# Window attention before two MLPs: scores of 64x64 blocks on quarters of the array

## The chip, the cores and the metric

One core of a Trainium2 chip (trn2). Its engines are TensorE (PE in the profile, with its weight loads as PEld), VectorE (DVE), ScalarE (ACT), GpSimd (POOL) and SyncE (SP, whose queue issues nearly all transfers here). Matmul results go to PSUM, 8 banks of 128 partitions by 512 fp32 columns; only PE, DVE and ACT reach it. The metric is device microseconds of one execution.

## The reference

Sliding-window attention (batch 4, 8 heads, 576 positions, head size 64, window 64), then two MLPs over the 2304 tokens, 512 to 2048 to 512 wide. The first MLP's activation is the square of the positive part, the second's is ELU. All in fp32.

```python
scores = (1 / sqrt(64)) * q @ k.T
rel = pos[:, None] - pos[None, :]
scores = where((rel >= 0) & (rel < 64), scores, -1e9)
attn = exp(scores - max(scores)); attn = attn / (sum(attn) + 1e-9)
x = (attn @ v)            # heads side by side: [2304, 512]
x = square(maximum(x @ w_in1, 0)) @ w_out1
h = x @ w_in2
out = where(h > 0, h, exp(minimum(h, 0)) - 1) @ w_out2
```

## The kernel before, in words

The tokens are cut into five blocks `t` of 512, 256, 512, 512 and 512 (`BLOCKS`). The eight heads are taken as four pairs `p`; a *unit* `(t, p)` is one head pair in one block. `q` and `k` come with the two heads of a pair on partitions 0 to 63 and 64 to 127 (`D` = 64) and positions along the free dimension. A window of 64 queries (`WIN`) meets only the 128 keys that end with its own 64, so a block of 512 has 8 windows of 64 queries by 128 keys for each head.

**Loads** (`u_load`, line 327). q goes into a tile `qd` laid out in blocks on the diagonal: in window `b`, head `a` occupies its own 64 partitions and columns `a*64` to `a*64+63` and the rest is zero, so two transfers with 256-byte pieces bring it in. k keeps whole lines with 64 positions ahead of the block, v comes in two arrangements. `load_to` issues them on SP a unit ahead. There are two q tiles, `qd0` and `qd1`, one for even and one for odd pairs.

**Scores** (`u_S`, line 369). One product a window: the weights are the 128x128 block-diagonal q of both heads, the moving operand is the 128 keys, contracted over all 128 partitions. Four windows share a PSUM bank `pa` (pool `ps_a`, two banks; block 0 uses the four banks of `ps_o`). A 128x128 result holds one window: 64 queries of the first head above 64 of the second. DVE adds the mask and takes the minimum (`tensor_tensor_reduce`, shown as CUSTOM_DVE), ACT takes the exponential with its sum, and the rows are divided by their sums on DVE, in block 1 on ACT. `mask[1]` is the mask of a window that begins a sequence; the 64 keys before it belong to another sequence.

**Transposes and the product with V** (`u_T`, line 413; `u_PV`, line 426). Each 128x128 is transposed on PE and copied to `pt` by ACT; then each window and head has a product of 64 columns on one half of the array's columns (`pa<-pt,vr`, 128*64 in the profile). `u_V2` does this for two units one after the other.

**First MLP, blocks 0 to 2.** For each of 16 column blocks `j` of the hidden layer, `m_h` (line 471) makes the first product `ph` (12 matmuls; each operand is split in two fp32r parts and three of their products are summed) in a bank of pool `ps_h` (two banks); ACT applies Relu and Square, ACT and DVE split the result into `gs`; `m_out` (line 490) adds the second product into four accumulators `o` in `ps_o` (12 matmuls). The main loop (lines 924 to 969) writes `m_h` two steps ahead of `m_out`, and puts among them the units of the next block: those of block 1 in block 0's loop, those of block 2 in block 1's, and those of blocks 3 and 4 from the end of block 1's through block 2's. `decode` and `slot` put conversions of the weights (fp64 to split fp32, sums of quarters for a fast matrix product) on DVE and ACT in between. Blocks 3 and 4 and the second MLP follow with seven products in place of eight (`stepw`, `step`, `prod2`; banks `px` from `ps_h`, `py` from `ps_a`, `po` from `ps_o`).

**Order.** A planner that simulates the engines chooses the order of each engine's instructions from the program order and the dependencies, at build time; each engine then runs its own queue in order. `tc.issue_after(x)` keeps what is written within it behind `x` in that order. `last["pe"]` and its like remember instructions for this. A tile with the same `tag` takes the place of an older one and waits until that is no longer used.

## Time and profile before

| | us |
|---|---|
| median of 3 runs (lowest to highest) | 830.05 (828.53 to 830.63) |
| the profiled execution's own time | 830.28 |
| its span, first to last instruction | 828.5 |

| engine | busy us | share of the span | instructions |
|---|---|---|---|
| PE | 813.0 | 98% | 4908 |
| PEld | 743.3 | 90% | 4908 |
| DVE | 666.4 | 80% | 1747 |
| ACT | 571.8 | 69% | 1353 |
| POOL | 5.8 | 1% | 21 |

How to read the profile: the busy time of PE includes pipelined matmuls whose ends are modelled, so the starts of instructions are what is compared. Most DVE and ACT instructions go through one helper and stand under its line, 53; they are told apart by the tiles that they write and read, as `pb<-pa,mask`. Line 467 holds both products of the first MLP (`ph<-xs,w` and `o<-gs,w`), 379 the scores, 420 the transposes, 433 the product with V.

### The profile page before, as it was taken

The page shows a single profiled execution, that of the slowest core. Times are in us where ns is not written, and L with a number is a line of the kernel's source. Part 1 is how long each engine was busy: PE and PEld are TensorE (multiplying, and loading weights), DVE is VectorE, ACT ScalarE, POOL GpSimd, SP SyncE. Part 2 cuts the span into 40 slices and gives each one's busy share as a digit, 9 for nine tenths or more (in the row PEclk, how much of TensorE's full clock was granted, in tenths as well). Part 3 has the DMA queues.
Part 4 walks back from the last instruction along what each step waited for, and adds up shares of the span by engine and source line. Part 5 has one row for each costly group of instructions (what it writes and reads, how often), then busy time and mean ns, then how long its engine had stood idle before and what let it go on. Part 6 is the DMA issues. An engine that isn't in the chain of part 4 may idle for free.

```text
span 828.5 us, 14865 instructions
## 1 busy us (share of the span) xinstructions
PE 813.0 (98%) x4908; PEld 743.3 (90%) x4908; DVE 666.4 (80%) x1747; ACT 571.8 (69%) x1353; POOL 5.8 (1%) x21
## 2 busy tenths in 40 slices
PE   6899999999999999999999999999999999999998
PEld 5687889998888887888888899999999999999998
DVE  7999995999689898989994767699666898576875
ACT  6787975678678777887773567766477756577552
POOL 2000000000000000000000000000000000000000
PEclk9999999999999999999999999999999999999999
DMA  9997334759467669999988696878987877887832
GB/s 303 386 394 266 110 110 131 228 191 295 158 217 213 234 213 361 338 379 353 333 296 276 230 336 253 303 269 274 311 268 263 305 260 228 268 279 270 299 118 58
DMA packets 121613, 214.90 MB, mean 259 GB/s; under 512 B 46144, under 2 KB 68928, under 8 KB 113088
## 3 DMA queue, kind: packets, MB, share of 16 engines
q1 hardware_dynamic: 120704, 213.75, 75.6%
q8 instruction: 39, 0.64, 0.3%
q14 instruction: 38, 0.31, 0.1%
q10 hardware_dynamic: 832, 0.20, 0.1%
HBM read 160.43 MB, written 53.48 MB: 258 GB/s over the span
## 4 chain that ended last, share of the span: by engine, by line
PE 90%; DMA 6%; SPq 2%; ACT 2%; issue 0%; DVE 0%; ACTq 0%
PE o L467 22%; PE po L883 20%; PE px L685 14%; PE ph L467 12%; PE py L685 10%; PE po L685 6%; PE pa L379 3%; DMA wraw<-in_moe_w_out_dram 2%; PE pa L433 2%; PE pa L420 1%; DMA wd<-w 1%; PE px L883 1%; DMA wraw<-in_moe_w_in_dram 1%; DMA qd<-in_q_dram 1%; DMA wd<-tl 1%; SPq L342 0%
## 5 line engine op out<-in xcount | busy, mean ns | idle before, releaser
L467 PE MATMUL o<-gs,w 128*128 128x512 f32 (+1 forms) x960 | 216.3, 372 | 0.0
L467 PEld LDWEIGHTS o<-gs,w 128*128 128x128 f32 x960 | 166.4, 189 | 29.2 <-ACT gs L53 0.3
L883 PE MATMUL po<-g,wr 128*128 128x384 f32 (+1 forms) x972 | 168.6, 333 | 0.0
L883 PEld LDWEIGHTS po<-g,wr 128*128 128x128 f32 x972 | 167.4, 188 | 0.0
L467 PE MATMUL ph<-xs,w 128*128 128x512 f32 (+1 forms) x576 | 126.8, 361 | 2.8 <-ACT xs L53 2.2
L53 ACT ACTIVATE g<-gr 128x384 fp32r<-128x384 f32 x168 | 86.9, 524 | 55.5 <-PE po L883 49.6
L467 PEld LDWEIGHTS ph<-xs,w 128*128 128x128 f32 x576 | 94.9, 190 | 17.9 <-ACT xs L53 2.7
L53 DVE TENSOR_TENSOR g<-gr,g 128x384 fp32r<-128x384 f32 x168 | 90.0, 552 | 16.1 <-ACT g L53 15.1
L685 PE MATMUL px<-xo,wr 128*128 128x384 f32 x432 | 83.8, 334 | 0.0
L685 PEld LDWEIGHTS px<-xo,wr 128*128 128x128 f32 x432 | 75.8, 188 | 0.3
L53 ACT ACTIVATE sy<-px 128x384 f32<-128x384 f32 x69 | 33.8, 490 | 42.5 <-PE px L685 42.0
L53 DVE TENSOR_SCALAR y<-y 128x256 uint32<-128x256 uint32 (+4 forms) x162 | 55.7, 366 | 6.8 <-ACT y L53 6.2
L53 ACT ACTIVATE pb<-pb,nm 128x128 f32<-128x128 f32 x144 | 55.8, 391 | 4.2 <-DVE nm L53 4.0
L685 PE MATMUL po<-xo,wr 128*128 128x384 f32 x288 | 56.2, 334 | 0.0
L685 PE MATMUL py<-xo,wr 128*128 128x384 f32 x288 | 55.7, 334 | 0.0
L53 DVE TENSOR_TENSOR gr<-sy,py 128x384 f32<-128x384 f32 x48 | 26.6, 554 | 35.6 <-PE py L685 23.3
L53 DVE TENSOR_TENSOR gr<-gr 128x384 f32<-128x384 f32 x96 | 52.2, 553 | 0.5
L685 PEld LDWEIGHTS po<-xo,wr 128*128 128x128 f32 x288 | 50.5, 188 | 0.0
L685 PEld LDWEIGHTS py<-xo,wr 128*128 128x128 f32 x288 | 50.5, 188 | 0.0
L53 DVE TENSOR_TENSOR gs<-g,gs 128x512 fp32r<-128x512 f32 (+1 forms) x64 | 39.7, 621 | 11.7 <-ACT gs L53 11.2
L685 PE MATMUL px<-xo,w 128*128 128x512 f32 x192 | 46.6, 390 | 0.7 <-ACT tl L53 0.7
L685 PEld LDWEIGHTS px<-xo,w 128*128 128x128 f32 x192 | 36.0, 188 | 8.6 <-ACT tl L53 1.2
(91 smaller groups left out, 1205.0 us busy)
## 6 DMA issues: line engine op xcount, KB each, us to landing
wr<-wd SPq DMA_DIRECT2D x66, 1024.0 KB, 6.0
wr<-wd SPq DMA_DIRECT2D x24, 768.0 KB, 4.8
wd<-tl SPq DMA_DIRECT2D x59, 256.0 KB, 3.8
w<-wd SPq DMA_DIRECT2D x56, 256.0 KB, 5.1
wd<-wo SPq DMA_DIRECT2D x46, 256.0 KB, 4.9
wd<-xs SPq DMA_DIRECT2D x39, 256.0 KB, 3.0
wraw<-in_moe_w_in_dram SPq DMA_DIRECT2D x16, 512.0 KB, 8.3
vr<-in_v_dram SPq DMA_DIRECT2D x16, 512.0 KB, 5.4
```

What stands on the lines that cost most here:

```text
L53: r = fn(*a, **kw)
L379: nc.tensor.matmul(out=ps[:, i * P:(i + 1) * P], lhsT=qr[:, b0 + i].rearrange("p a x -> p (a x)"), rhs=kr[:, o:o + P], start=True, stop=True,)
L420: nc.tensor.transpose(out=ps[:, i:i + P], in_=pb[:, i:i + P], identity=ident)
L433: nc.tensor.matmul(out=ps[d, b * WIN:(b + 1) * WIN], lhsT=vr[:, b % 2, b // 2, d], rhs=pt[:, d], start=True, stop=True,)
L467: last["pe"] = nc.tensor.matmul(out=ps, lhsT=a[x], rhs=b[y], start=(first and i == 0), stop=(final and i == 2))
L685: last["pe"] = nc.tensor.matmul(out=ps[:, :NH], lhsT=w[:, wr_, c * P:(c + 1) * P], rhs=x[:, xr_, c], start=first and n == 0, stop=final an ...
L883: last["pe"] = nc.tensor.matmul(out=ps[m][:, lo:hi], lhsT=w[:, y, m * P:(m + 1) * P], rhs=s[:, x, lo:hi], start=k in fresh and p == 0 and ...
```

## The change

From block 1 on (block 0 keeps the old scores as `u_S0`):

- q is loaded with whole lines by one transfer, the two heads on their own 64 partitions, no zeros.
- A score product has 64 queries of one head as weights and that head's 64 partitions as contraction: it uses a 64x64 quarter of the array. Head `a` decides the rows and the PSUM bank, the even or odd window `e` the columns and the partitions of the result. Sixteen products make a full unit, in groups of four in the order (1,1), (0,0), (1,0), (0,1), held in one chain: the first comes behind the last 13 remembered PE instructions and each other behind the one before it.
- A 128x128 result now holds two windows of one head. Masks are chosen for the two together, and a third mask is made on POOL after block 0's units. The product with V picks its columns accordingly.
- The banks of `ps_a` and `ps_h` are shared out anew by `share`: three and one from the first step of block 1's loop to the last but one of block 2's, two and two before and after.

```diff
     wts = pool(ctx, "wts", 1)
-    ps_a = pool(ctx, "ps_a", 2, space=PSUM)
-    ps_h = pool(ctx, "ps_h", 2, space=PSUM)
     ps_o = pool(ctx, "ps_o", 1, space=PSUM)
+    mid = ctx.enter_context(ExitStack())
+    ps = {}
+
+    def share(a, h):
+        mid.close()
+        ps["a"] = pool(mid, "ps_a", a, space=PSUM)
+        ps["h"] = pool(mid, "ps_h", h, space=PSUM)
+
+    share(2, 2)
     at = pool(att, "at", 2)
...
+
+    def more_masks():
+        nc.gpsimd.tensor_copy(mask[2], mask[0])
+        nc.gpsimd.memset(mask[2][WIN:P, 0:WIN], NEG)
+        nc.gpsimd.tensor_copy(mask[1][WIN:P], mask[0][WIN:P])
...
+    recent = []
     raw = {}
+
+    def note():
+        recent[:] = [*recent[-12:], last["pe"]]
...
         if "q" in parts:
-            if early:
+            if t:
+                qr = at.tile([P, 2 * NMAX], F32, tag=f"qd{p % 2}", name="qr", bufs=1)
+            elif early:
                 qr = sc.tile([P, 2 * NQ, 2, D], F32, tag="gs", name="qd", bufs=GB)
                 zero_q(qr, nc.gpsimd)
             else:
                 qr = qd[p % 2]
             r0["q"] = qr
-            for a in range(2):
+            if t:
+                nc.sync.dma_start(out=qr[:, :n], in_=q[p, :, t0:t0 + n])
+            for a in range(0 if t else 2):
                 w = slice(a * D, (a + 1) * D)
                 nc.sync.dma_start(
...
+    def u_S(u, alloc):
+        t, p = u
+        if t == 0:
+            return u_S0(u, alloc)
+        qr, kr = raw[u]["q"], raw[u]["k"]
+        nm = at.tile([P, 2 * NQ], F32, tag="nm", name="nm")
+        sm = at.tile([P, 2 * NQ], F32, tag="sm", name="sm")
+        rc = at.tile([P, 2 * NQ], F32, tag="rc", name="rc")
+        m = BLOCKS[t] // P
+        sb = [alloc() for _ in range(2)]
+        held = list(recent)
+        for i in range(m):
+            for a, e in ((1, 1), (0, 0), (1, 0), (0, 1)):
+                d, o = slice(a * D, (a + 1) * D), (2 * i + e) * WIN
+                with ExitStack() as line:
+                    for ins in held:
+                        line.enter_context(tc.issue_after(ins.ins))
+                    last["pe"] = nc.tensor.matmul(
+                        out=sb[a][e * WIN:(e + 1) * WIN, i * P:(i + 1) * P],
+                        lhsT=qr[d, o:o + WIN], rhs=kr[d, o:o + P], start=True, stop=True,
+                    )
+                held = [last["pe"]]
+        note()
+        for n0 in range(0, 2 * m, 4):
+            pb = at.tile([P, 4 * P], F32, tag="pb", name="pb", bufs=4)
+            for n in range(n0, n0 + 4):
+                a, i = divmod(n, m)
+                c = slice((n - n0) * P, (n - n0 + 1) * P)
+                g = [(T0[t] + (2 * i + e) * WIN) % S == 0 for e in range(2)]
+                vec.tensor_tensor_reduce(
+                    out=pb[:, c], in0=sb[a][:, i * P:(i + 1) * P],
+                    in1=mask[g[0] + 2 * g[1]],
+                    scale=-SCALE, scalar=3.0e38, op0=ALU.add, op1=ALU.min,
+                    accum_out=nm[:, n:n + 1],
+                )
+                last["act"] = act.activation(
+                    out=pb[:, c], in_=pb[:, c], func=AF.Exp,
+                    bias=nm[:, n:n + 1], scale=-1.0, accum_out=sm[:, n:n + 1],
+                )
+            r = rc[:, n0:n0 + 4]
+            vec.tensor_scalar(
+                out=r, in0=sm[:, n0:n0 + 4], scalar1=1.0e-9, scalar2=None, op0=ALU.add
+            )
+            vec.reciprocal(out=r, in_=r)
+            for n in range(n0, n0 + 4):
+                c = slice((n - n0) * P, (n - n0 + 1) * P)
...
                 last["dve"] = vec.tensor_scalar(
-                    out=pb[:, c], in0=pb[:, c], scalar1=rc[:, b:b + 1], scalar2=None, op0=ALU.mult
-                )
-            prb[u, b0] = pb
+                    out=pb[:, c], in0=pb[:, c], scalar1=rc[:, n:n + 1], scalar2=None, op0=ALU.mult
+                )
+            prb[u, n0] = pb
...
             for i in range(0, m * P, P):
-                nc.tensor.transpose(out=ps[:, i:i + P], in_=pb[:, i:i + P], identity=ident)
+                last["pe"] = nc.tensor.transpose(
+                    out=ps[:, i:i + P], in_=pb[:, i:i + P], identity=ident
+                )
+            note()
...
-        for b, pt in enumerate(pts):
+        for b in range(len(pts)):
+            i, e = divmod(b, 2)
             for a in range(2):
-                d = slice(a * D, (a + 1) * D)
-                nc.tensor.matmul(
-                    out=ps[d, b * WIN:(b + 1) * WIN],
-                    lhsT=vr[:, b % 2, b // 2, d], rhs=pt[:, d], start=True, stop=True,
-                )
+                d, x = slice(a * D, (a + 1) * D), slice(e * WIN, (e + 1) * WIN)
+                last["pe"] = nc.tensor.matmul(
+                    out=ps[d, b * WIN:(b + 1) * WIN], lhsT=vr[:, e, i, d],
+                    rhs=pts[a * len(pts) // 2 + i][:, x] if t else pts[b][:, d],
+                    start=True, stop=True,
+                )
+        note()
         return ps
...
-        ps = ps_h.tile([P, 512], F32, tag="h", name="ph")
+        ph = ps["h"].tile([P, 512], F32, tag="h", name="ph")
             mm3(
-                ps[:, :n],
+                ph[:, :n],
...
-    a_alloc = lambda: ps_a.tile([P, 512], F32, tag="a", name="pa")
+    a_alloc = lambda: ps["a"].tile([P, 512], F32, tag="a", name="pa")
...
-            return ps_h.tile([P, 512], F32, tag="h", name="px")
...
+    more_masks()
...
+        if (t, j) in ((1, 0), (TW, NJ - 2)):
+            share(*((3, 1) if t == 1 else (2, 2)))
```

In `bank`, `px` and `py` come from `ps["h"]` and `ps["a"]` likewise; `constants` makes the first two masks as before.

## Rows read from the trace of the kernel before

**Rows 1.** The page: busy time, share, instructions; granted clock by slices.

```profile
PE 813.0 (98%) x4908; PEld 743.3 (90%) x4908; DVE 666.4 (80%) x1747; ACT 571.8 (69%) x1353; POOL 5.8 (1%) x21
...
PEclk9999999999999999999999999999999999999999
```

**Rows 2.** The page: the chain that ended last, by engine and by line.

```profile
PE 90%; DMA 6%; SPq 2%; ACT 2%; issue 0%; DVE 0%; ACTq 0%
PE o L467 22%; PE po L883 20%; PE px L685 14%; PE ph L467 12%; PE py L685 10%; PE po L685 6%; PE pa L379 3%; DMA wraw<-in_moe_w_out_dram 2%; PE pa L433 2%; PE pa L420 1%; DMA wd<-w 1%; PE px L883 1%; DMA wraw<-in_moe_w_in_dram 1%; DMA qd<-in_q_dram 1%; DMA wd<-tl 1%; SPq L342 0%
```

**Rows 3.** Busy time by stretches (from:to, length, then each engine's busy us).

```profile
142.50:188.80 46.30, 46.30 (x481) 45.66 (x480) 42.91 (x143) 34.23 (x108) 0.00 (x0) 1.00 0.67 213
188.80:302.70 113.90, 113.90 (x826) 97.28 (x826) 96.08 (x404) 86.54 (x263) 0.00 (x0) 1.00 0.68 216
```

**Rows 4.** Line 379: passes, duration ns min/median/max, first and last start, products.

```profile
L379 PE MATMUL pa<-kr,qd x224: 270/275/275, 45.6 to 286.9; 128*128 128x128 f32 x112
```

**Rows 5.** PE in order of time (start, length, merged instructions).

```profile
168.71 1.60 PE L467 MATMUL ph<-xs,w 128*128 128x256 f32 x12
170.15 1.95 PE L379 MATMUL pa<-kr,qd 128*128 128x128 f32 x16
171.85 1.68 PE L467 MATMUL o<-gs,w 128*128 128x256 f32 x12
173.37 1.60 PE L467 MATMUL ph<-xs,w 128*128 128x256 f32 x12
```

**Rows 6.** PE in order of time, 184 to 190 us.

```profile
183.73 1.24 PE L467 MATMUL ph<-xs,w 128*128 128x256 f32 x9
184.90 2.08 PE L433 MATMUL pa<-pt,vr 128*64 128x64 f32 x64
186.92 0.62 PE L467 MATMUL ph<-xs,w 128*128 128x256 f32 x3
187.38 1.60 PE L467 MATMUL o<-gs,w 128*128 128x256 f32 x12
```

**Rows 7.** PE in order of time, 153.8 to 158.5 us.

```profile
154.40 1.15 PE L433 MATMUL pa<-pt,vr 128*64 128x64 f32 x32
155.49 1.46 PE L467 MATMUL o<-gs,w 128*128 128x256 f32 x10
156.88 1.15 PE L433 MATMUL pa<-pt,vr 128*64 128x64 f32 x32
```

**Rows 8.** PE and ACT in order of time, 199 to 208 us.

```profile
200.76 3.82 PE L467 MATMUL ph<-xs,w 128*128 128x512 f32 x16
...
205.19 0.58 ACT L53 ACTIVATE g<-ph 128x512 f32<-128x512 f32 x1
```

**Rows 9.** PE and ACT in order of time, 274 to 283 us.

```profile
278.45 0.84 PE L467 MATMUL o<-gs,w 128*128 128x512 f32 x3
...
280.49 0.57 ACT L53 ACTIVATE g<-ph 128x512 f32<-128x512 f32 x1
```

**Rows 10.** Groups by line and shape (count, busy us, mean ns).

```profile
L53 ACT ACTIVATE pb<-pb,nm 128x128 f32<-128x128 f32 x144 | 55.8, 391 | 4.2 <-DVE nm L53 4.0
...
L53 DVE CUSTOM_DVE_ANT_0 pb<-pa,mask 128x128 f32<-128x128 f32 x112 | 26.1, 286 | 1.9 <-PE pa L379 1.8
...
L53 DVE DVE_READ_ACCUMULATOR2_ANT nm<- 128x1 f32 x144 | 12.1, 84 | 0.0
```

**Rows 11.** Line 342, q's transfers (issue ns); SP's waits (total us, times, longest).

```profile
L342 SPq DMA_DIRECT2D qd<-in_q_dram x40: 595/627/1682, 1.7 to 258.8; - x40
...
SPq L342 <- PE pa L379: 25.6, 9, 9.3
```

**Rows 12.** PE in order of time, 300.5 to 313.6 us.

```profile
302.88 6.42 PE L467 MATMUL o<-gs,w 128*128 128x512 f32 x27
...
313.44 0.50 PE L685 MATMUL px<-xo,w 128*128 128x512 f32 x1 [0.73 <-ACT tl L53]
```

**Rows 13.** Line 379 in the last stretch: PE busy (passes), PEld busy (loads).

```profile
188.80:302.70 113.90, 16.83 (x128) 16.74 (x128) 1.00 0.68 216
```

More of the change, by code (lines that the diff above doesn't have):

```diff
@@ L95, in window_attention_then_two_mlps @@
     ident = cst.tile([P, P], F32, name="ident")
-    mask = [cst.tile([P, P], F32, name=f"mask{i}") for i in range(2)]
+    mask = [cst.tile([P, P], F32, name=f"mask{i}") for i in range(3)]
     qd = [at.tile([P, 2 * NQ, 2, D], F32, tag=f"qd{i}", name=f"qd{i}", bufs=1) for i in range(2)]
@@ L108, in constants @@
     def constants():
-        for m in mask:
+        for m in mask[:2]:
             nc.gpsimd.memset(m, 0.0)
@@ L367, in banks, with u_S0 @@
         return [(b, min(4, nb - b)) for b in range(0, nb, 4)]
-    def u_S(u, alloc):
+    def u_S0(u, alloc):
         t, p = u
@@ L402, in u_S @@
                 c, b = slice(i * P, (i + 1) * P), b0 + i
-                if t == 1:
-                    act.activation(
-                        out=pb[:, c], in_=pb[:, c], func=AF.Copy, scale=rc[:, b:b + 1]
-                    )
-                    continue
                 last["dve"] = vec.tensor_scalar(
@@ L411, in u_S @@
             prb[u, b0] = pb
+    def u_S(u, alloc):
[44 more added lines that the diff above has]
+                c = slice((n - n0) * P, (n - n0 + 1) * P)
+                if t == 1:
+                    act.activation(
+                        out=pb[:, c], in_=pb[:, c], func=AF.Copy, scale=rc[:, n:n + 1]
+                    )
+                    continue
+                last["dve"] = vec.tensor_scalar(
+                    out=pb[:, c], in0=pb[:, c], scalar1=rc[:, n:n + 1], scalar2=None, op0=ALU.mult
+                )
+            prb[u, n0] = pb
@@ L469, in mm3 @@
             )
+        note()
     def m_h(t, j):
@@ L484, in m_h @@
         s = sc.tile([P, 2, NMAX], F32R, tag="gs", name="gs", bufs=GB)
-        act.activation(out=g[:, :n], in_=ps[:, :n], func=AF.Relu)
+        act.activation(out=g[:, :n], in_=ph[:, :n], func=AF.Relu)
         act.activation(out=g[:, :n], in_=g[:, :n], func=AF.Square)
@@ L664, in bank @@
         if k == "x":
-            return ps_h.tile([P, 512], F32, tag="h", name="px")
+            return ps["h"].tile([P, 512], F32, tag="h", name="px")
         if k == "a":
-            return ps_a.tile([P, 512], F32, tag="a", name="py")
+            return ps["a"].tile([P, 512], F32, tag="a", name="py")
         return ps_o.tile([P, 512], F32, tag=f"o{k}", name="po")
```

## The prediction

> **What bounds the kernel now.** I read the page's busy line and clock row first, then the chain of work that ended last, then stretches of time, then the attention instructions by themselves. TensorE (PE) is busy for 813 of 828.5 us and its granted clock stands at nine tenths or more in every slice, so it runs at the upper of its two levels, 2.4 GHz [rows 1]. The chain is PE for 90% of the span, and the scores on line 379 are 3% of it in their own right [rows 2]. By stretches [rows 3]: in the loops of block 1 (142.5 to 188.8 us) and block 2 (to 302.7), PE is busy without a break, while VectorE (DVE) is at 42.9 of 46.3 and 96.1 of 113.9 us, and ScalarE (ACT) lower still. So a microsecond of PE work taken out there is worth about a microsecond, as long as nothing that feeds PE becomes late. Block 1's loop has only 3.4 us of free DVE time, and that is the place to watch.
>
> **What the scores cost.** Line 379 has 224 PE records on the `pa` banks for 112 products: each fp32 product is two passes [rows 4]. From block 1 on there are 4 head pairs with 4 products (block 1) and 12 with 8 products (blocks 2 to 4), 4x4 + 12x8 = 112. Price of one pass: 16 score passes and 12 second-product passes run from 170.15 to 173.37 us, 3.22 us; twelve such passes take 168.71 to 170.15 = 1.44 us, so 16 score passes take 1.78 us, 0.111 each, and nothing is lost on entering or leaving [rows 5]. A full unit is 1.78 us, a half unit 0.89.
>
> **What the new scores cost.** No row shows a product on a 64x64 quarter. The nearest is the product with V on line 433, which already runs on 64-column halves of the array. From 183.73 to 187.38 us stand 64 of its passes and 12 first-product passes (9 + 3): 3.65 - 1.44 = 2.21 us [rows 6]. From 154.40 to 156.88 stand 32 of them and 10 others of 0.12: 2.48 - 1.20 = 1.28 us [rows 7]. The difference, 0.93 us for 32 passes, is 0.029 us a pass, and a fixed 0.35 us is left for each chain, for changing the shape of the array and back. A V pass moves 64 columns, half of a score pass: alone it should take 0.111/2 = 0.055. It takes about half of that, so two halves work side by side.
>
> The new chain of a full unit has 16 quarter products, 32 passes, each of 128 moving columns, 0.111 us alone. One at a time that is 3.55 us, two at a time 1.78, four at a time 0.89; plus 0.35 for the chain. Bounds for a full unit, therefore: 1.24 to 3.9 us, against 1.78. The V rows exclude "one at a time", since halves do overlap there. Between two and four I take four: the halves of V fill the array's width completely (0.029 against the ideal 0.028), and the four quarters of a group cover the array without overlapping, so I carry over the same 4% of loss: 0.93 + 0.35 = 1.28 us, 0.50 less than now. A half unit has 16 passes: 0.46 + 0.35 = 0.81 against 0.89, 0.08 less. Sum: 12 x 0.50 + 4 x 0.08 = 6.3 us, of which 4.0 falls in block 2's loop, where 128 of the 224 passes stand, eight full units [rows 13]; the half units belong to block 0's loop, and the last four full ones to the rest. That is far below the 17.8 us of DVE time that are free in block 2's loop, and at most 2.0 of the 3.4 in block 1's [rows 3].
>
> One rule speaks against "four". The V rows would look the same if passes had to start strictly in program order: the second pass of one product beside the first of the next is already two at a time [rows 6]. The Trainium skill, TensorE: Matmul & The Clock Gate, section Part 3 (packing small matmuls), says that matmuls start and end in program order and that only weight loads are pulled ahead. By that, a full unit takes 1.78 + 0.35 = 2.13 us here. The same section has a model in which each further tile adds about 4 ns to one matmul; by that, as an estimate, it takes 8 x (0.111 + 0.012) + 0.35 = 1.33 us.
>
> **The other edits.** *One bank for the first product* (between the second first product of block 1 and the end of block 2, 29 of them): the next `ph` may not start until ACT's Relu has read the last. At its worst now, 16 `ph` passes stand in a row from 200.76 to 204.41, 3.65/16 = 0.228 each, so a second product begins at 200.76 + 12 x 0.228 = 203.5 while the first's Relu ends at 205.77: 2.3 us too early for one bank [rows 8]. Where a second product of 12 x 0.228 = 2.7 us lies between, it covers a Relu like the one that ends at 281.06, 2.6 us after PE has gone on at 278.45 [rows 9]. That is nearly all of the cover: with 0.5 us less of scores around it there is no slack. Bounds: 0 (the second product goes first and Relu is in time) to 4.8 us (0.3 at each of block 2's 16 first products: the slack of 0.1 less the scores' 0.5, rounded). I take 1.0, a short wait at three or four of them.
>
> *The held chain and the two banks it takes at once.* PE takes its instructions in order, so while a chain waits for q, k or its second bank, the first and second products behind it wait too. The cover is the third `pa` bank. DVE's pass over a bank of four windows takes 4 x (0.286 + 0.084) = 1.5 us [rows 10]. Bounds: 0 to 1.5 us for each of eight units; I take 0.3 in all, because two chains in a row are separated by about one pair of products.
>
> *Softmax.* Tiles of 128x128 remain, holding two windows of one head in place of one window of two heads; the counts on DVE (112 reductions of 0.286) and ACT (exponentials at 0.391) do not change [rows 10]. Transposes and V products keep number and shape. Zero.
>
> *Loading q.* Two transfers with 256-byte pieces become one with whole lines: 32 issues of about 0.63 us on SP's queue become 16 [rows 11]. No q load after 10 us stands on the chain [rows 2], the loads run a unit ahead, and SP issues far less than PE works: between 0 and 0.3 us gain; I take 0. If a chain does stand late, its buffer is released late, and SP's queue behind that load (k, v, weights, stores) waits, as it does now in total 25.6 us behind line 379 [rows 11].
>
> *The third mask.* Three POOL instructions. POOL's 21 instructions take 5.8 us, 0.28 each, and it is idle for 99% of the span [rows 1]. Block 1's first scores run at 45.6 us [rows 4], and the masks come right after block 0's units; that idle POOL time hides them, and without it they would cost about 0.8 us. Zero.
>
> *The join at 303 us.* After the last V product PE fills 302.88 to 309.3 with 27 passes of the second product, just until the next stage's products, and waits 0.73 us at 313.4 [rows 12]. What it waits for there (weights loaded into attention's freed space, x made by ACT and DVE) starts from that last V product, so it moves with it. If instead it came from a fixed rate of DMA, all of the gain after 190 us would be lost here.
>
> **Sum.** -6.3 + 1.0 + 0.3 = -5.0 us. The profiled execution took 830.28 us around a span of 828.5, and the median of the runs is 830.05; so 825.3 us.
>
> **The rivals.** *Two at a time* (slower). Strict order of starts, or quarters that share a column strip not loading weights side by side. A full unit costs 1.78 + 0.35, a half 0.89 + 0.35: +0.35 x 16 = +5.6, with the 1.3 of waits 837.2 us. For it: nothing in the trace uses row halves, and a product's two passes share their quarter. Against it: in the V rows both halves are as full as they can be. The point that decides is 0.045 us a pass, (1.78 - 0.35)/32; above that the change loses. *The single bank takes the gain back* (no change). Its upper bound: -6.3 + 4.8 = -1.5, 828.8 us. For it: the 2.6 against 2.7 us above; against it: Relu also starts earlier where ACT waits for PE. *A better overlap* (faster still): 0.89 a unit, no waits for banks, and an entry and exit that cost half, since a chain's 0.35 was read off V products with 64 columns: 12 x 0.72 + 4 x 0.27 = 9.7, so 820.6 us.
>
> **How the numbers follow.** A time within 0.3% (2.5 us) of now can't be told from no change by this measurement. Chances: forecast 0.56 (its own range 822 to 828.5), better overlap 0.07, the single bank 0.19 (826.5 to 832), two at a time 0.18 (834 to 840). Faster by over 0.3%, below 827.6: 0.52 + 0.07 + 0.03 = 0.62. Slower, above 832.5: 0.17 + 0.02 = 0.19. The rest, 0.19, is within. The range leaves out most of "two at a time" and the far side of the better overlap: 820.5 to 833.
>
> **What would show it.** In the profile after, a score chain of a full unit should hold PE for about 1.3 us from its first pass to the next whole-array product, with starts in groups of four; 2.1 would mean two at a time. PE's idle rows should show `ph` waiting for ACT `g` for about 1 us in total; several us there would be the single bank. DVE's busy time in block 1's loop should come near the loop's length. The forecast is wrong if the passes average over 0.045 us, or if the stage from 303 us starts no earlier than now.

## The result, and the profile after

The changed kernel takes 837.32 us (median of 6 runs, 836.35 to 841.80) where the kernel before, on the same chip, takes 830.30: 7 us more, or a ratio of 1.0096 with a 95% interval of [1.0068, 1.0124]: slower by 6 to 10 us. The forecast was 825.3, faster, and its range ended at 833. "Two at a time", the rival on the slower side, had named 837.2, but not for the reason that the trace shows.

The page of the changed kernel: busy time with shares, then the chain that ended last by engine and by line.

```profile
PE 815.0 (98%) x5132; PEld 732.9 (88%) x5132; DVE 666.6 (80%) x1747; ACT 574.1 (69%) x1353; POOL 6.4 (1%) x24
...
PE 85%; DVE 5%; DMA 5%; ACT 4%; issue 1%; SPq 0%; DVEq 0%; ACTq 0%
PE po L961 20%; PE o L544 19%; PE px L763 14%; PE ph L544 10%; PE py L763 10%; PE po L763 6%; DMA wd<-tl 3%; DVE y L53 2%; PE pa L508 2%; PE pa L491 2%; DVE pb L53 1%; PE pa L445 1%; ACT pb L53 1%; PE px L961 1%; DMA wd<-xs 1%
```

Beside [rows 1, 2]: PE's busy time rose by 2 us although the scores became cheaper, and DVE and ACT, 0% and 2% of the chain before, now hold 9% of it. The scores have gone from 3% of the chain to 1%. So the scores did get cheaper, and the time is lost elsewhere. Where, the stretches tell. Block 1's and block 2's loops, taken from the end of block 0's second product, in the kernel before:

```profile
135.30:200.60 65.30, 65.30 (x619) 63.63 (x618) 56.88 (x199) 48.67 (x153) 0.00 (x0) 1.00 0.71 227
200.60:312.30 111.70, 111.70 (x790) 94.40 (x789) 95.35 (x373) 84.13 (x244) 0.00 (x0) 1.00 0.66 212
```

The same stretches of the changed kernel (from:to, length, then busy us of PE, PEld, DVE, ACT and POOL, then the granted clock):

```profile
133.50:200.80 67.30, 66.42 (x707) 60.91 (x706) 59.52 (x238) 50.29 (x167) 0.00 (x0) 1.00 0.70 221
200.80:319.50 118.70, 115.21 (x916) 91.68 (x915) 102.96 (x397) 89.25 (x260) 0.00 (x0) 0.99 0.66 224
```

177.0 us became 186.0. PE had no idle time there and now has 4.4 us (0.88 + 3.49). DVE's work in the two loops rose from 152.2 to 162.5 us, while its whole busy time stayed: of the passes of scores after block 0's, 160 of 224 stood in these loops before, 384 of 448 now, so the scores of two full units that block 0's loop used to take come later. The first loop begins 1.8 us earlier and block 2's ends 7.2 us later.

The three attention groups on PE over the whole span (count of passes, busy us, mean ns, then idle time before them). First the kernel before:

```profile
L379 PE MATMUL pa<-kr,qd 128*128 128x128 f32 x224 | 29.3, 274 | 0.0
L420 PE MATMUL pa<-ident,pb 128*128 128x128 f32 x144 | 23.1, 279 | 0.5 <-ACT pt L53 0.5
L433 PE MATMUL pa<-pt,vr 128*64 128x64 f32 x576 | 21.4, 228 | 1.4 <-ACT pt L53 1.0 <-DVE xs L53 0.2
```

And the changed kernel:

```profile
L491 PE MATMUL pa<-ident,pb 128*128 128x128 f32 x144 | 26.1, 284 | 2.1 <-DVE pb L53 1.9
L508 PE MATMUL pa<-pt,vr 128*64 128x64 f32 x576 | 24.5, 229 | 1.2 <-ACT pt L53 0.9 <-DVE xs L53 0.3
L445 PE MATMUL pa<-kr,qr 64*64 64x128 f32 x448 | 18.0, 277 | 0.3 <-DVE xr L53 0.3
```

Scores fall by 11.3 us of busy time. But the same 144 transposes take 3.0 us more and the same 576 V passes 3.1 us more: they now stand in short pieces. (A group's busy time counts the tail of its last instruction, so many pieces weigh more here than by start times, where it is 1.8 and 2.3 us; a table by starts follows with the first experiment.)

PE in order of time, changed kernel: a score chain, the turn from block 1 to block 2, a piece of block 2, the last V product, and the next stage's first product.

```profile
135.79 2.44 PE L544 MATMUL o<-gs,w 128*128 128x256 f32 x19
138.16 1.10 PE L445 MATMUL pa<-kr,qr 64*64 64x128 f32 x32
139.19 1.69 PE L544 MATMUL ph<-xs,w 128*128 128x256 f32 x12
140.72 1.48 PE L544 MATMUL o<-gs,w 128*128 128x256 f32 x11
...
199.52 0.43 PE L445 MATMUL pa<-kr,qr 64*64 64x128 f32 x2
199.88 1.91 PE L544 MATMUL o<-gs,w 128*128 128x256 f32 x11
201.72 1.10 PE L445 MATMUL pa<-kr,qr 64*64 64x128 f32 x30
203.06 0.52 PE L491 MATMUL pa<-ident,pb 128*128 128x128 f32 x2 [0.23 <-DVE pb L53]
204.88 1.43 PE L544 MATMUL ph<-xs,w 128*128 128x512 f32 x5 [1.30 <-ACT g L53]
...
281.49 1.10 PE L445 MATMUL pa<-kr,qr 64*64 64x128 f32 x30
284.27 0.72 PE L491 MATMUL pa<-ident,pb 128*128 128x128 f32 x3 [1.68 <-DVE pb L53]
284.74 0.48 PE L544 MATMUL ph<-xs,w 128*128 128x512 f32 x1
285.06 0.27 PE L491 MATMUL pa<-ident,pb 128*128 128x128 f32 x1
285.08 4.35 PE L544 MATMUL ph<-xs,w 128*128 128x512 f32 x11
289.27 2.70 PE L544 MATMUL o<-gs,w 128*128 128x512 f32 x11
...
301.31 1.15 PE L508 MATMUL pa<-pt,vr 128*64 128x64 f32 x30
302.38 1.19 PE L544 MATMUL ph<-xs,w 128*128 128x512 f32 x4
...
314.30 1.52 PE L763 MATMUL px<-xo,w 128*128 128x512 f32 x6
```

The next stage's first product in the kernel before:

```profile
309.14 1.52 PE L685 MATMUL px<-xo,w 128*128 128x512 f32 x6
```

Five things are to be seen. First, a whole chain of 32 quarter passes takes 1.03 us from its start to the next product; the 19 products ahead of it take 2.37 for 19 x 0.12 = 2.28 and the 12 behind it 1.53 for 1.44, so it costs 1.21 in all, where the prediction had 1.28. Its passes start in groups of four within 0.02 us, and from the second group on the groups stand 0.109 us apart, as single full-array passes stand 0.111 apart in the kernel before. Second, "held in one chain" is not "in one piece": at least four of the twelve full chains are cut after their first product (x2, then other work, then x30), and the two lone passes cost 0.36 us. Third, PE waits: 1.30 us for the Relu that empties the one `ph` bank, 1.68 for softmax. Fourth, the 11 passes from 285.08 take 4.19 us, where they take 11 x 0.228 = 2.5 elsewhere. Fifth, the last V product is done at 302.38, half a microsecond earlier than before [rows 12], but the stage after block 2 starts at 314.30 and not at 309.14: more of the first MLP's own products are left by then.

The fourth of these is the clock. Changed kernel, the stretches before and during those passes (the 1.00 and 0.53 are the granted clock):

```profile
282.00:285.70 3.70, 2.02 (x30) 1.51 (x23) 3.70 (x18) 3.61 (x12) 0.00 (x0) 1.00 0.19 74
285.70:289.30 3.60, 3.60 (x11) 2.77 (x10) 3.60 (x19) 1.27 (x4) 0.00 (x0) 0.53 0.72 273
```

After a stretch in which PE stood idle for 1.68 us the granted clock falls to 0.53, most of that stretch at the lower level, 1.2 GHz, and 1.7 us more are gone. PE's waits by cause, changed kernel, whole span (total us, times, longest):

```profile
PE ph L544 <- ACT g L53: 2.2, 4, 1.3
...
PE pa L491 <- DVE pb L53: 1.9, 2, 1.7
```

Of the 2.2 us, 1.6 us in two waits lie in the two loops.

### The profile page after: what moved, and what is told of

It is laid out like the page before. It is cut to its first block, busy times and chain, and to the rows that moved or that the text cites. A ratio compares the mean times of both kernels' runs of the same rounds, so it can differ in the third digit from the quotient of the medians.

```text
span 835.1 us, 15288 instructions
## 1 busy us (share of the span) xinstructions
PE 815.0 (98%) x5132; PEld 732.9 (88%) x5132; DVE 666.6 (80%) x1747; ACT 574.1 (69%) x1353; POOL 6.4 (1%) x24
## 4 chain that ended last, share of the span: by engine, by line
PE 85%; DVE 5%; DMA 5%; ACT 4%; issue 1%; SPq 0%; DVEq 0%; ACTq 0%
PE po L961 20%; PE o L544 19%; PE px L763 14%; PE ph L544 10%; PE py L763 10%; PE po L763 6%; DMA wd<-tl 3%; DVE y L53 2%; PE pa L508 2%; PE pa L491 2%; DVE pb L53 1%; PE pa L445 1%; ACT pb L53 1%; PE px L961 1%; DMA wd<-xs 1%
## 5 line engine op out<-in xcount | busy, mean ns | idle before, releaser
L544 PE MATMUL o<-gs,w 128*128 128x512 f32 (+1 forms) x960 | 214.1, 372 | 1.1 <-DVE gs L53 0.5
L544 PEld LDWEIGHTS ph<-xs,w 128*128 128x128 f32 x576 | 95.5, 191 | 23.1 <-ACT g L53 3.7
```

What stands on the lines that cost most here:

```text
L544: last["pe"] = nc.tensor.matmul(out=ps, lhsT=a[x], rhs=b[y], start=(first and i == 0), stop=(final and i == 2))
```

## The experiments

Three theories stood: the **shares** of the PSUM banks cost the time, or the **held order** does, or the **quarters** themselves do. Ratios below are to the kernel before on the same chip, with the 95% interval. Of the eighteen expectations only those of d1_single_ph, a5_no_hold and c_s24_nohold name a range that holds the measured time; b3_before_held, b1_one_quarter and c_s2 miss one by less than 0.4 us, and the other twelve miss all of theirs, nine of them on the slow side.

**The shares alone, and one bank alone.** Two kernels have the scores of the kernel before:

```diff
+        if (t, j) in ((1, 0), (TW, NJ - 2)):
+            share(*((3, 1) if t == 1 else (2, 2)))   # a3_share_alone
+            share(*((2, 1) if t == 1 else (2, 2)))   # d1_single_ph
```

> The kernel before, with nothing but the new share of banks (three for attention and one for the first product from the second product of block 1 to the last but one of block 2). Theory 1, the shares: slower than before by about as much as the change was, 834 to 838 us, with V stretches cut as in the changed kernel (more than 15 in blocks 1 and 2) and new waits of the first product for ACT. Theory 2, the held chain, and theory 3, the quarters: within 2 us of before, 829 to 832 us.

> The kernel before, with one bank for the first product in the same stretch as in the change, but two for attention (one bank stands empty). The share of three and one alone took before to 842.36 us. Theory A, the single bank of the first product does it (ph waits for the square of the Relu, 9.4 us of such waits in that run): 836 to 842 us. Theory B, the third attention bank does it (it lets transposes and passes of V alternate, 17 stretches of V in blocks 1 and 2 for 7 before): 829 to 833 us, with V in stretches of 32 passes or more.

Measured: 842.36 us, 1.0130 [1.0112, 1.0148], and 840.76 us, 1.0122 [1.0091, 1.0153]. Three and one alone make the kernel before slower than the whole change does. Taking the bank from the first product costs about as much by itself; the third attention bank changes what the time is lost in, as the table below shows, and not how much. Stretches of d1_single_ph:

```profile
133.30:200.50 67.20, 66.08 (x623) 64.04 (x622) 57.38 (x219) 49.52 (x163) 0.00 (x0) 1.00 0.67 209
200.50:325.00 124.50, 116.34 (x807) 96.99 (x806) 103.04 (x390) 87.77 (x254) 0.00 (x0) 1.00 0.66 214
```

9.3 us of PE idle (1.12 + 8.16), and its waits there name the releaser:

```profile
PE ph L474 <- ACT g L53: 6.5, 3, 3.0
...
PE px L692 <- ACT g L53: 2.7, 1, 2.7
```

9.2 us, in four waits. One of them, PE in order of time, d1_single_ph:

```profile
199.71 2.91 PE L474 MATMUL ph<-xs,w 128*128 128x512 f32 x12
...
204.66 0.93 PE L474 MATMUL o<-gs,w 128*128 128x512 f32 x3
208.59 3.01 PE L474 MATMUL ph<-xs,w 128*128 128x512 f32 x12 [3.00 <-ACT g L53]
```

And on ACT in the same time:

```profile
204.93 0.44 ACT L53 ACTIVATE y<-praw 128x256 f32<-128x256 f32 x1 [2.16 <-DMA praw<-in_moe_w_in_dram]
205.27 0.39 ACT L53 ACTIVATE pb<-pb,nm 128x128 f32<-128x128 f32 x1
...
207.58 0.39 ACT L53 ACTIVATE pb<-pb,nm 128x128 f32<-128x128 f32 x1
207.87 0.19 ACT L53 ACTIVATION_READ_ACCUMULATOR pb<-pb,nm 128x1 f32 x1
207.96 0.58 ACT L53 ACTIVATE g<-ph 128x512 f32<-128x512 f32 x1
```

The first product's last pass started before 202.46; its Relu ran at 207.96, behind weight decoding that had waited 2.16 us for a transfer and behind seven exponentials. With two banks such a late Relu is harmless, with one it stops PE.

Where each kernel's time goes can be counted. Each PE instruction is charged with the time from its start to the next one's start, less PE's idle time between; the columns are the kernel before, the change, a3_share_alone and d1_single_ph, one profiled execution each (us, whole span):

| | before | change | three and one | one bank |
|---|---|---|---|---|
| scores of blocks 1 to 4 | 22.7 | 16.7 | 23.6 | 22.8 |
| transposes | 15.7 | 17.5 | 17.7 | 15.5 |
| products with V | 20.3 | 22.6 | 23.1 | 20.9 |
| first MLP (`ph` and `o`) | 317.8 | 322.1 | 318.9 | 319.4 |
| idle | 5.6 | 10.3 | 11.5 | 13.6 |
| all else | 436.2 | 435.8 | 436.3 | 436.7 |

The change saves 6.0 us of scores and loses 4.6 to idle, 4.1 to transposes and V products and 4.3 to the first MLP's products, 1.7 of these by the half clock and some 1.5 right before quarter chains. Three and one alone has the same two losses without any quarter: 5.8 of idle and 4.7 of transposes and V products. One bank alone has 8.0 of idle and 0.4 of the other. So the third attention bank turns waits into pieces. A transpose with a V product right behind it takes about 0.22 us to that one's start, where one with a transpose behind it takes 0.12; there are 3 such turns before, 14 in the change, 13 with three and one alone and 2 with one bank alone.

**The order alone.** The kernel before, its full-array scores behind the last 13 noted PE instructions and each other:

```diff
+        held = list(recent) if t else []
...
+                    for ins in held:
+                        line.enter_context(tc.issue_after(ins.ins))
```

> The kernel before, with nothing but the order: its 128x128 scores of blocks 1 and 2 stand behind the last 13 noted PE instructions and behind one another. Theory 2, the held chain: two units leave block 0's loop, block 2 ends 4 to 8 us later, 834 to 838 us. Theory 1, the shares: 829 to 832 us, though the first full unit moves behind 130 us. Theory 3: 829 to 832 us.

Measured: 832.33 us, 1.0025 [1.0013, 1.0036]. The order costs 2 us there: clear of zero, but too little to be the cause by itself. The reverse, the changed kernel with no order on the scores (a5_no_hold), and with V's products ordered too (a4_hold_v):

> The changed kernel, shares of three and one, with no order on the scores. In the kernel before the held order alone cost 1.6 to 2 us. If it costs the same here: 834 to 837 us. If the order is what keeps the chains whole and the quarters' gain with it: 838 to 842 us.

> The changed kernel, with the V products of blocks 1 and 2 also in one chain behind the last 13 noted PE instructions, so that fewer transposes come between them; shares stay 3 to 1. Theory 1a, the loss is the cutting of V products and transposes themselves (V 12.2 to 14.7 us and T 8.5 to 11.7 us of PE time): 832 to 834 us. Theory 1b, the loss is the single bank's and the transposes' waits, whatever the order: 836 to 838 us. Theories 2 and 3: 836 to 839 us.

Measured: 841.91 us, 1.0165 [1.0140, 1.0190], and 841.23 us, 1.0121 [1.0095, 1.0146]. With one `ph` bank the order helps, as the second branch of a5_no_hold's expectation had it. Part of that is the order within the chain, which goes too: in a5_no_hold many passes start two at a time, 16 of them take 1.02 us where 16 of a held half unit take 0.60, and the scores take 19.7 us by starts for 16.7. Whole V chains do not help: in a4_hold_v PE is idle for 8.0 us of the same two loops instead of 4.4. This fits pieces that were filling waits.

**Two banks each.** The changed kernel without the `share` calls, with the held chain (a1_two_two), without it (a8_22_nohold), and without it and with the units of blocks 3 and 4 a step earlier (f1_22_early):

```diff
-            share(*((3, 1) if t == 1 else (2, 2)))      # all three
-        held = list(recent)
+        held = []                                       # a8, f1, and no order within the chain
-        i0 = i - NJ * TW + 2
+        i0 = i - NJ * TW + 3                            # f1
```

> The changed kernel with two banks for attention and two for the first product all through (the calls that share them out 3 to 1 are gone); quarters and the held chain stay. Theory 1, the shares: the third attention bank lets transposes come in between the passes of a V product (18 stretches of V passes in blocks 1 and 2 after, 7 before), and the single bank makes the first product wait for the square of the Relu. Then this kernel loses most of the 9 us that the stretch of blocks 1 and 2 grew by, V stretches go back to 7 or so, PE ph<-ACT g waits (2.2 us) go, and the time is 826 to 831 us. Theory 2, the held chain: scores that are ordered behind the last 13 PE instructions leave block 0's loop (first full unit at 138 us, 104 us before), and VectorE's work of two units moves into blocks 1 and 2. Then the first full unit stays past 130 us and the time is 834 to 838 us. Theory 3, the quarters themselves (each chain in and out of the quarters costs TensorE about 0.35 us): no change, 836 to 838 us.

> The changed kernel with two banks each all through and no order on the scores at all. With two each and the held chain the second product of block 2 ended at 302.3 us (312.3 before), but the last unit's scores, transposes and V products came after it, and the time was 847.96 us. Theory A, the held chain puts the attention late: without it the last units are done sooner, the tail of 21.7 us shrinks to under 10, and the time is 832 to 838 us. Theory B, a unit that needs both attention banks for its scores at once lets nothing else of attention start, whatever the order: the last unit still stands behind block 2, 843 to 848 us.

> The changed kernel with two banks each, no order on the scores, and the units of blocks 3 and 4 handed to the planner one step earlier. Without the last it took 840.65 us: the second product of block 2 ended at 307.8 us, 4.6 before the kernel before, but the next stage began at 318 because attention was not done. If the late start is the cause, the next stage begins some 3 us earlier or more: 832 to 838 us. If the two banks' turnover is the cause: 839 to 842 us.

Measured: 847.96 us, 1.0203 [1.0187, 1.0218]; 840.65 us, 1.0127 [1.0107, 1.0148]; 848.66 us, 1.0231 [1.0204, 1.0258]. The theory of the shares had 826 to 831 us for a1_two_two; giving the bank back does not bring the time back, and the loss is not in waits of `ph`. Stretches of a1_two_two:

```profile
197.50:302.30 104.80, 104.80 (x794) 83.41 (x793) 78.34 (x313) 71.88 (x209) 0.00 (x0) 1.00 0.59 197
302.30:324.00 21.70, 10.20 (x115) 7.83 (x113) 18.99 (x87) 15.23 (x52) 0.00 (x0) 0.66 0.46 163
```

PE runs through block 2's loop without a break, then stands for half of 21.7 us. In order of time, a1_two_two:

```profile
305.55 1.61 PE L445 MATMUL pa<-kr,qr 64*64 64x128 f32 x30 [0.40 <-DVE nm L53]
310.64 1.94 PE L491 MATMUL pa<-ident,pb 128*128 128x128 f32 x8 [3.49 <-DVE nm L53]
...
315.47 3.68 PE L508 MATMUL pa<-pt,vr 128*64 128x64 f32 x64
323.97 2.93 PE L763 MATMUL px<-xo,w 128*128 128x512 f32 x6 [4.82 <-DMA w<-wd]
```

In the kernel's code a unit's chain takes both attention banks at once, and no transpose or V product gets one until DVE has read them; that attention falls behind for this reason is a reading, for no run gives it quarters without it. What the trace shows is that eight of the twelve chains are cut after their first product here, that the last unit is left over with nothing beside it, and that the next stage's weights, whose space the code frees when attention is done, come late: PE's wait for them is 4.8 us here, 7.3 in a8_22_nohold and 6.0 in f1_22_early. The last two moved the tail and did not remove it; the earlier step missed its expectation outright.

**Other shares.** Three and one in block 2 alone with the held chain (c_s2), and, with no order on the scores, from the fifth or ninth first product of block 2 on:

```diff
-        if (t, j) in ((1, 0), (TW, NJ - 2)):
-            share(*((3, 1) if t == 1 else (2, 2)))
+        sw = {(2, 0): (3, 1), (TW, NJ - 2): (2, 2)}   # (2, 4): c_s24_nohold; (2, 8): c_s28_nohold
+        if (t, j) in sw:
+            share(*sw[t, j])
```

> The changed kernel with two banks each in block 1 and three and one in block 2 alone. In the change, block 1's second product ended 0.2 us later than before, with two each all through 3.1 us earlier; block 2's stretch took 118.7 us for 111.7. If the bank costs in block 1 too: about 3 us come back, 833 to 835 us. If what is won in block 1 is lost again in block 2 (the units come in later): 836 to 840 us.

> The changed kernel with no order on the scores, and with the share of three and one only from the fifth first product of block 2 on (two each before that). If the quarters save what the prediction summed (6 us) and the loss sits in the stretch with one ph bank, which is now a third as long as in the change: 826 to 831 us. If the tail of the last units decides, as with two each all through: 838 to 848 us. If the loss of the single bank is all in block 2: 836 to 840 us.

> As the run before, with the share of three and one only from the ninth first product of block 2 on. Less waiting of ph than there: 825 to 830 us if the last units still end within block 2; 835 to 845 us if they come after it.

Measured: 835.18 us, 1.0067 [1.0042, 1.0091]; 838.26 us, 1.0099 [1.0073, 1.0125]; 854.20 us, 1.0299 [1.0271, 1.0327]. c_s2 is the best of the kernels with quarters, 2 us below the change by the medians (the intervals overlap), and still slower than before. Its block 1 loop has no PE idle, its block 2 has 4.7 us:

```profile
133.00:197.50 64.50, 64.50 (x708) 60.44 (x707) 57.42 (x220) 47.78 (x157) 0.00 (x0) 1.00 0.68 219
197.50:315.00 117.50, 112.78 (x900) 88.70 (x899) 101.16 (x406) 88.71 (x263) 0.00 (x0) 0.99 0.67 226
```

Among the kernels without order on the scores, three and one from block 1 on gives 1.0165 (a5_no_hold), from the fifth first product of block 2 on 1.0099, from the ninth on 1.0299, and never 1.0127 (a8_22_nohold): a later change helps at first and then does harm. In c_s28_nohold one `ph` wait alone is 5.0 us.

**The order of quarters within the chain.**

```diff
-        for i in range(m):
-            for a, e in ((1, 1), (0, 0), (1, 0), (0, 1)):
+        for a, e in ((1, 1), (0, 0), (1, 0), (0, 1)):
+            for i in range(m):
```

> The changed kernel with the order of the chain turned: all products of one quarter in a row, then those of the next (the same products and banks). If quarters overlap only when neighbours in the order lie on different quarters, passes of a full unit go from 0.027 us to about 0.11 each, a chain takes 3.5 to 3.9 us instead of 1.2, and the 12 full and 4 half units add about 12 x 2.6 + 4 x 1.3 = 36 us of TensorE time: 850 to 873 us. If the queue of TensorE reaches far enough ahead to overlap quarters 16 passes apart: about 837 us.

Measured: 849.69 us, 1.0219 [1.0200, 1.0238]. A full chain, b1_one_quarter:

```profile
137.09 2.56 PE L445 MATMUL pa<-kr,qr 64*64 64x128 f32 x32
139.58 1.69 PE L544 MATMUL ph<-xs,w 128*128 128x256 f32 x12
```

2.49 us for 32 passes, against 1.03 in the order of the change, on the same quarters and banks. So the overlap depends on neighbours in the order. It is 2.49 and not 3.55: by their starts, passes of one quarter stand 0.109 us apart, and around each turn to the next quarter two quarters run side by side. By the count of starts all the scores of blocks 1 to 4 take 18.3 us more than in the change, and the time rose by 10 to 12 (ratios, medians): so a microsecond of PE was not worth a whole one in this kernel.

**Four banks in turn.** No fixed share: attention and the first product draw from one pool of four (all through, the last stages too), for the change (e1_rot4), with V's products held (e4_rot4_holdv), and for the kernel before (e6_before_rot4).

```diff
-    share(2, 2)
+    ps["a"] = ps["h"] = pool(mid, "ps_b", 4, space=PSUM)
```

> The changed kernel with no fixed share: attention and the first product take the four banks in turn, so a first product waits for the fourth bank back and not for the last Relu. Quarters and held chain as in the change. If the loss is the wait for one bank of the first product (10.8 us when that bank alone was taken from the kernel before), ph waits for ACT g nearly vanish and the quarters' gain is left: 822 to 829 us. If giving turns makes first products wait for attention's readers instead: 836 to 845 us.

> As the run before, with the V products also in one chain behind the last 13 noted PE instructions (23 stretches of V passes in the written order of the whole kernel for 41). If the cutting of V products costs (V passes took 14.7 us in blocks 1 and 2 after, 12.2 before): 1 to 3 us less than that run. If the cuts only fill gaps, as a V chain held in the changed kernel did (841.23 for 837.32 us): the same or some us more.

> The kernel before, with attention and the first product taking the four banks in turn. It is the control: if turns are good or bad in themselves, this run shows it without the quarters. Expected within 4 us of before, 826 to 834 us; then the difference between the two runs with turns is what the quarters and their order bring, -4 to -6 us by the theory of the single bank, 0 or more if the quarters' saving is not real.

Measured: 851.97 us, 1.0240 [1.0218, 1.0263]; 840.95 us, 1.0116 [1.0086, 1.0146]; 845.51 us, 1.0163 [1.0145, 1.0182]. Turns cost 14 us without any quarter, so these runs say little of the quarters: with turns the quarters and their order are 0.8% slower than without (e1_rot4 against e6_before_rot4), and with V's products held 0.5% faster. That holding V's products saves 11 us here and nothing with three and one is not explained by any run. In e1_rot4 the `ph` waits for the Relu are gone from the list of waits, and waits for transposes' copies, softmax and g's parts stand in their place.

**The Relu on VectorE.** For the change (q6_relu_dve), the kernel before with one bank (q7_single_relu_dve), and the kernel before (q8_before_relu_dve, the control):

```diff
-        act.activation(out=g[:, :n], in_=ph[:, :n], func=AF.Relu)
+        vec.tensor_scalar(out=g[:, :n], in0=ph[:, :n], scalar1=0.0, scalar2=None, op0=ALU.max)
```

> The changed kernel with the Relu on VectorE in place of ScalarE. Theory A: 826 to 833 us, better than the change's 837.3. Theory B: 836 to 845 us, since VectorE then carries 29 more operations of about 0.6 us in blocks 1 and 2.

> The kernel before with one bank for the first product and two for attention, and the Relu that empties that bank on VectorE in place of ScalarE (the square stays on ScalarE). With the Relu on ScalarE this took 840.76 us; first products waited for Relus that ended up to 6 us after the product, behind exponentials and weight decoding in ScalarE's queue. Theory A, ScalarE's queue is the cause: the waits of ph for g shrink by more than half, 831 to 836 us. Theory B, any queue that the Relu shares with attention's and the weights' work gives the same: 838 to 846 us, with waits for DVE in place of ACT.

> The kernel before, two banks each, with the Relu on VectorE in place of ScalarE. Control of the single bank with that move (849.87 us). If ScalarE's queue was what made the single bank dear, the bank costs little here: 845 to 850 us. If the bank costs about 11 us whoever empties it: 837 to 841 us.

Measured: 847.35 us, 1.0224 [1.0204, 1.0244]; 849.87 us, 1.0251 [1.0228, 1.0273]; 842.46 us, 1.0141 [1.0120, 1.0161]. The move costs 12 us by itself. Against its control the single bank costs 1.1% with the Relu on VectorE and 1.2% with it on ScalarE. So, as far as the intervals tell, ScalarE is not special: one bank costs about the same whichever of the two queues empties it.

## Why the prediction was wrong

**The score term held.** The prediction had 1.28 us for a full unit's chain, four quarters at a time; 1.21 was measured for an uncut one, and by starts the scores save 6.0 us for the 6.3 forecast (some 1.5 of it is lost again at the products right before the chains). "Two at a time" is out: 1.03 + 0.18 is far from 2.13, and 1.03/32 = 0.032 us a pass is below the deciding 0.045. Its 837.2 was met by chance. The Trainium skill, TensorE: Matmul & The Clock Gate, section Part 3, says that matmuls start and end in program order. The prediction worked out 2.13 us by that, with the two passes of a product as neighbours, and the trace, with starts in groups of four, does not bear that out. The same section's model with 4 ns for each further tile gave 1.33 as an estimate, nearer to the trace. That the order of the products matters, b1_one_quarter shows.

**The step that failed is "one bank for the first product": +1.0, bounds 0 to 4.8.** Alone it costs 10 us (d1_single_ph), in four PE waits of 9.2 us together, twice the upper bound; with the third attention bank, as in the change, 11 us (a3_share_alone). The bound took a small wait at each of block 2's products, from the one usual distance between a product and its Relu [rows 9], and left out block 1's. The worst distance lay in view: [rows 8] had a Relu ending 2.3 us too late for one bank, at the turn from block 1 to block 2, and it was noted and priced away as covered. In d1_single_ph the price is set by the tail: ACT works in order, and a Relu behind a decode that waits for a transfer ends 6 us after its product (202.46 to 208.54). With two banks this hides. The prediction's own sign, `ph` waiting for ACT `g` for about 1 us, would not have found this in the changed kernel: such waits are 1.6 us in its two loops, while the share's cost stands in the table as idle of other kinds and as transposes and V products in pieces.

**"The held chain and the two banks": +0.3 was too little in both halves.** The order alone costs 2 us in the kernel before. Without the third bank attention falls behind, and in a1_two_two a tail of 21.7 us stands after block 2, half of it idle; the claim on two banks at once is the likely reason. The prediction named the third bank as the cover and did not ask what the kernel would pay without it. So the banks are a choice between two losses: give `ph` one and PE waits for Relus, give attention two and the next stage waits for attention. That the two heads' chains need two banks is in the kernel's code; the Trainium skill, TensorEngine Tiling (Array Packing), Gotcha 1, says of row tiles in general that they write to different PSUM banks. No run here put both heads into one bank.

**Transposes and V products at "keep number and shape, zero" were wrong in time.** Number and shape kept, place did not: 4.1 us more by starts. It is the share of the banks that does this, for a3_share_alone has 4.7 of it without a quarter and d1_single_ph 0.4: with a third bank the planner puts V products among transposes, and each turn costs its share of the 0.35 us that the prediction itself had read from V chains. That entry was priced once for each score chain and not for a chain cut in two.

**Not foreseen: the half clock** after PE's wait that ended at 284.27 us, 1.7 us.

**"The join at 303 us" failed too.** The next stage was to move with the last V product. That product was done 0.5 us earlier, and the next stage began 5.2 us later, because the first MLP itself was behind.

**"A microsecond of PE is worth a microsecond" holds only while nothing that feeds PE becomes late**, as the prediction said. It did become late, so no kernel with quarters got below the one before. At three and one they bring 0.3% less time with the held order (a3_share_alone to the change, 1.0130 to 1.0096; 6.0 us in the profiled executions) and 0.35% more without it (a5_no_hold, 1.0165); the intervals overlap. What they would bring with five banks for these two uses, no run can say.

So the forecast of -5.0 was -6.3 and +1.3, and the trace has -6.0 and +13.0 (4.6 of idle, 4.1 of transposes and V products, 4.3 at the first MLP's products), with 0.4 less elsewhere: 6.6 us more. Open: the runs' costs do not add up from kernel to kernel (the order costs 2 us in one and saves 5 in another), and since giving the bank back brings its own loss, no run takes the share's cost out of the changed kernel. No kernel tried beats the kernel before.

## What to carry to other kernels

Price a buffer that is taken away by the latest consumer in the loop, not by the usual one: look through the whole loop for the reader that stands behind a transfer in its engine's queue. When a cheaper instruction needs its operands' space all at once, ask first which neighbour pays for that space, and try the share alone, without the gain: that one run (a3_share_alone) had most of the answer. Chains ordered behind each other can still be cut by other work, and a cut pays the entry again.

## What the runs showed of the hardware

- Products on four 64x64 quarters of the array, neighbours in the order on different quarters, start four within 0.02 us, and the next four 0.109 us later, where full-array passes of the same 128 columns stand 0.111 us apart [rows 5]: four at a time, though the two passes of each fp32 product share a quarter. Over a whole chain that is 0.032 us a pass. With all products of a quarter in a row it is 2.49/32 = 0.078.
- Two lone quarter passes between full-array products hold PE for 0.36 us, a third of what all 32 take.
- The granted clock fell to 0.53 in a stretch of 3.6 us that followed PE idle of 1.68 us in one wait, within a stretch that was busy for 2.02 of 3.70 us; in the same stretch of time the kernel before had no idle and kept 1.00. A long wait does not always do this: around the 3.00 us wait of d1_single_ph that ended at 208.59 the granted clock stayed at 1.00.
